# Decay attention and a squared-ReLU FFN: the attention in plain float32 on quarters of the array, one chunk per stretch

## The chip, the cores and the metric

The kernel runs on one core of a Trainium2 chip. The metric is the device time of one execution in microseconds; lower is better. The kernel before was timed three times: 644.21, 644.75 and 645.5 us, median 644.75 us. The profile that is read below comes from an execution of its own.

## The reference

Two operations follow each other. The first is a causal attention with a decay per head, in blocks of 64 positions, for 4 batches, 8 heads, 768 positions and 64 features per head. Its result is the input of a feed-forward network over 3072 tokens.

```python
intra = np.einsum('bhic,bhjc->bhij', qb, kb) * Dmask[None]      # Dmask: lam ** (i - j) for i >= j, else 0
intra = np.einsum('bhij,bhjd->bhid', intra, vb)
inter = np.einsum('bhid,bhde->bhie', qb * lam_pow[None], kv_state)
out[:, :, sl] = intra + inter
kv_state = lam_block[None, :, None, None] * kv_state + np.einsum('bhsd,bhse->bhde', kb_dec, vb)
...
h = np.maximum(x @ w_in, 0.0)        # x: 3072 x 512, w_in: 512 x 2048
return (h * h @ w_out).astype(np.float32)      # w_out: 2048 x 512
```

All inputs and outputs are float32. The FFN's weights arrive as 64-bit words and are turned into float32 on the chip.

## The kernel before

**Tiling.** The kernel works in chunks of 128 positions (`C`), six per batch, 24 in all. `CHUNKS` lists first the four chunks with number 0, one of each batch, and then the rest batch by batch. Three chunks make a token tile of 384 tokens, and there are eight tiles (`TILES`). For each tile the attention of its three chunks writes `x` as a high part `xh` and a low part `xl` in the type float32r, and the FFN then runs 16 steps (`ffn`, one per 128 hidden features).

**The FFN.** One step is twelve matmuls of 384 columns into a PSUM bank `h` (L509: `xh` by `wih`, `xl` by `wih`, `xh` by `wil`), a ReLU and a square on ACT and DVE with a split into `gh` and `gl` (L523 to L530), and nine matmuls of 512 columns that accumulate into three banks `os_`, one per chunk (L515, L516, L518). In the first two tiles the weights of each step are also unpacked and split, on ACT and DVE (`weights`, L265 to L290); from the third tile on they lie ready.

**The attention.** Every chunk is worked in two units of four heads (index `q`). The first nine chunks (`PLAIN`) use float32 matmuls: `unit_plain`, with scores on halves of the array's rows (L319, 64x128 of it), the state's update on halves of its columns (L342), and the result from the state on the whole array (L368) and from the scores on halves of its columns (L371). A float32 matmul shows as two MATMUL records, called passes here. The other 15 chunks (`SPLIT`) use `unit_split`: queries, keys, values, scores and state are each split into a high and a low part in float32r by copies on ACT and subtractions on DVE (L408 to L425, L443, L444); the scores (L432) and the result (L474, L475) are float32r matmuls on the whole array, and the parts of the result are added again on ACT and DVE (L439, L440, L481 to L488). The state's update (L452) is a float32 matmul there, too.

**What sets the order.** `Plan.order` runs once at build time. It takes each operation with an engine, an estimated duration, a key (when it is due) and its buffers, and it hands out buffers and writes one fixed order per engine. Where the estimates leave PE idle in the first 45 us, it puts in filler matmuls on zeros (L241). Buffers for the first phase (`EARLY`) and for the split attention (`LATE`) share the same memory. Two PSUM banks are kept for `h`, and six are shared by the attention and the FFN's accumulators. All loads and stores are issued from SP's queue.

Of the kernel before, what the change touches and what calls it, by code (L numbers as in the profile page):

```python
# [19 lines left out]
P = 128  # L20
# [7 lines left out]
PK = 1536  # L28
# [5 lines left out]

# [6 lines left out]
N_PLAIN = 9  # L41
PLAIN, SPLIT = CHUNKS[:N_PLAIN], CHUNKS[N_PLAIN:]

# [9 lines left out]
class Op:  # L53
    def __init__(self, eng, dur, key, fn, deps, bufs, after, lat, early):
        self.eng, self.dur, self.key, self.fn, self.deps, self.bufs, self.after, self.lat, self.early = (
            eng, dur, key, fn, deps, bufs, after, lat, early)
        self.start = self.end = None


class Plan:  # L60
    LAT = {"PE": 0.25, "ACT": 0.15, "DVE": 0.12, "POOL": 0.12, "SP": 2.0}
    PORT = ("DVE", "POOL")
# [7 lines left out]
    def op(self, eng, dur, key, fn, deps=(), bufs=(), after=(), lat=None, early=None):  # L70
        o = Op(eng, dur, key, fn, [d for d in deps if d is not None], list(bufs), [d for d in after if d is not None], lat or self.LAT[eng], early)
        for b in o.bufs:
            b.left += 1
        self.ops.append(o)
        return o

    def order(self, pe_slow, fill, begin):

# [9 lines left out]
        done, filled, early = [], 0, sum(o.early is True for o in self.ops)  # L88
        while any(ready.values()):
            best = None  # L90
            for e, ops in ready.items():
                can = []
                for o in ops:
                    t = max([free[e]] + [d.end + d.lat for d in o.deps])
                    want = {}
                    for b in o.bufs:
                        if b.slot is None:
                            want[b.kind] = want.get(b.kind, 0) + 1
                    ok = o.early is not False or not early
# [16 lines left out]

# [8 lines left out]
            dur = o.dur * (2.0 if o.eng == "PE" and t < pe_slow else 1.0)  # L125
            o.start, o.end = t, t + dur
# [11 lines left out]
            early -= o.early is True  # L138
# [7 lines left out]


SLOTS = {
# [4 lines left out]
EARLY = ("pnt", "diag0", "diag1", "st", "m")  # L153
LATE = ("pkt", "ab", "ka", "vv", "pp", "z", "zl", "ss0", "ss1")

FIRST, SLOW_STEP, LAG, BEGIN2, SECOND, STEP, PE_SLOW, FILL_END, FILL = 18.0, 6.5, 16, 9.0, 1.5, 4.8, 4.9, 45.0, 0.215

BEHIND = 12  # L160

SPARE = 0.8
# [3 lines left out]
def kernel(ctx: ExitStack, tc: tile.TileContext, pn, pk, lamx, w, out):  # L166
# [3 lines left out]
    phase = ExitStack()  # L170
    plan = Plan()
    for k, n in SLOTS.items():
        plan.kind(k, n)


    shapes = {
        "bank": ([P, 512], F32), "h": ([P, 512], F32),
        "gh": ([P, N], F32R), "gl": ([P, N], F32R), "g": ([P, N], F32), "ob": ([P, DM], F32),
        "s1": ([P, 4, C], F32), "vd": ([P, 4, D], F32), "us": ([P, 2, D], F32), "xr": ([P, 2, C], F32),
        "st": ([P, DM], U64), "m": ([P, DM], F32), "pnt": ([P, 4, 2, P], F32), "diag0": ([P, 2, P], F32), "diag1": ([P, 2, P], F32),  # L180
        "pkt": ([P, PK], F32), "ab": ([P, 4, 2, C], F32R), "ka": ([P, 4, C], F32R), "vv": ([P, 4, 2, D], F32R),
        "pp": ([P, 4, 2, C], F32R), "z": ([P, 2, 2, C], F32), "zl": ([D, 2, 2, C], F32),
        "ss0": ([P, 2, 2, 2, D], F32R), "ss1": ([P, 2, 2, 2, D], F32R), "hold": ([P, 2, D], F32)}
# [6 lines left out]
    make(ps, ("bank", "h"))  # L190
    make(const, [k for k in SLOTS if k not in EARLY + LATE + ("bank", "h", "x")])
    tiles["x"] = [[const.tile([P, NCC, N], F32R, name=f"{n}{i}") for n in ("xh", "xl")] for i in range(SLOTS["x"])]
    rdec = const.tile([P, NP, C], F32, name="rdec")

    flip, zero = tiles["g"][-1][:, 0:P], tiles["ob"][-1]
    lam, ej, ec = (tiles["g"][-1][:, P + 16 * i:P + 16 * i + n] for i, n in enumerate((H + NP, H, NP)))
    mask = const.tile([P, P], F32, name="mask")
# [3 lines left out]
    wol = [const.tile([P, DM], F32R, name=f"wol{f}") for f in range(NF)]  # L201

    wdec = const.tile([P, H], F32, name="wdec")
    lc = const.tile([P, NP], F32, name="lc")
    make(phase.enter_context(tc.tile_pool(name="early", bufs=1)), EARLY)

    def late():
        phase.close()
        pool = ctx.enter_context(tc.tile_pool(name="late", bufs=1, reuse_waits="tile"))
        pool.tile([P, 112], F32, name="space")  # L210
        make(pool, LATE)

        for k in ("ss0", "ss1"):
            for s in tiles[k]:
                nc.gpsimd.memset(s.bitcast(F32), 0.0)
# [4 lines left out]

    def start_tables():
        nc.scalar.dma_start(out=lam, in_=lamx)
        nc.vector.memset(zero, 0.0)
        nc.gpsimd.iota(ej, pattern=[[0, H]], base=MID, channel_multiplier=-1, allow_small_or_imprecise_dtypes=True)
        nc.vector.memset(ec, float(C))

# [4 lines left out]

        for d in tiles["diag0"] + tiles["diag1"]:
            nc.vector.memset(d, 0.0)

        nc.scalar.mul(tiles["g"][-1][:, P + 48:P + 52], zero[:, 0:4], 1.0)

        nc.gpsimd.tensor_tensor(out=wdec, in0=lam[:, 0:H], in1=ej, op=ALU.pow)
        nc.gpsimd.tensor_tensor(out=lc, in0=lam[:, H:H + NP], in1=ec, op=ALU.pow)

    def filler(i):  # L240
        nc.tensor.matmul(tiles["bank"][i][:, 0:P], zero[:, 0:P], zero[:, P:2 * P], start=True, stop=True)  # L241
# [3 lines left out]
    o_start = plan.op("POOL", 1.2, -99, start_tables, early=True)  # L245


    o_pow = plan.op("POOL", 3.0, -98, lambda: None, [o_start], early=True)
    wb, rps = Buf("m"), Buf("bank")

    def turned():
        for n in range(NP):
            nc.tensor.matmul(
                at(rps)[:, n * C:n * C + C], at(wb)[:, n * P:n * P + P], flip, start=True, stop=True)

    o = plan.op("DVE", 0.4, -5, lambda: nc.vector.tensor_copy(
        at(wb).rearrange("p (n h d) -> p n h d", n=NP, h=2), wdec.rearrange("p (n h) -> p n h", h=2).unsqueeze(3).broadcast_to([P, NP, 2, D])),
        [o_pow], [wb], early=True)
    o_turned = o = plan.op("PE", 0.9, 3, turned, [o], [wb, rps], early=True)
    o_rdec = plan.op("DVE", 0.6, 3, lambda: nc.vector.tensor_tensor(  # L260
        out=rdec, in0=at(rps).rearrange("p (n i) -> p n i", n=NP), in1=lam[:, H:H + NP].unsqueeze(2).broadcast_to([P, NP, C]), op=ALU.mult),
        [o], [rps], early=True)


    def weights(f, i, key):  # L265
# [9 lines left out]
        def add(eng, dur, fn, deps, bufs, lat=None):  # L275
            return plan.op(eng, dur, key, fn, deps, bufs, lat=lat, early=True)

        o = plan.op("SP", 1.95, key - 6, lambda: nc.sync.dma_start(out=at(st), in_=w[f, i]), [o_start], [st], early=True)
        o = add("ACT", 0.55, lambda: nc.scalar.activation(at(m), words(1).bitcast(F32), AF.Abs), [o], [st, m])  # L279
        o = add("DVE", 0.35, lambda: nc.vector.tensor_scalar(  # L280
            out=at(m), in0=at(m), scalar1=W_MIN, scalar2=W_MAX, op0=ALU.max, op1=ALU.min), [o], [m])
        o = add("DVE", 0.35, lambda: nc.vector.tensor_scalar(
            out=bits(), in0=bits(), scalar1=3, scalar2=0x3FFFFFF8, op0=ALU.logical_shift_left, op1=ALU.bitwise_and), [o], [m])
        o = add("DVE", 0.6, lambda: nc.vector.scalar_tensor_tensor(
            out=bits(), in0=words(1), scalar=0xC0000000, in1=bits(), op0=ALU.bitwise_and, op1=ALU.bitwise_or), [o], [st, m])
        o = add("DVE", 0.6, lambda: nc.vector.scalar_tensor_tensor(
            out=bits(), in0=words(0), scalar=29, in1=bits(), op0=ALU.logical_shift_right, op1=ALU.bitwise_or), [o], [st, m])
        oh = add("ACT", 0.55, lambda: nc.scalar.copy(hi, at(m)), [o], [m])  # L288
        ol = add("DVE", 0.6, lambda: nc.vector.tensor_tensor(out=lo, in0=at(m), in1=hi, op=ALU.subtract), [oh], [m])
        return oh, ol  # L290


    state, turn = {}, {}

    def in_turn(name, o):

# [5 lines left out]
    half = lambda h: slice(h * 64, h * 64 + 64)  # L302

    def unit_plain(b, c, q, x, col, key, behind=None):

        prs = slice(2 * q, 2 * q + 2)
        t, s1, vd, xr = Buf("pnt"), Buf("s1"), Buf("vd"), Buf("xr")

        def add(eng, dur, dk, fn, deps, bufs, name=None):
            o = plan.op(eng, dur, key + dk, fn, deps, bufs, early=True)  # L310
            return in_turn(name, o) if name else o

        load = add("SP", 1.7, -8, lambda: nc.sync.dma_start(out=at(t), in_=pn[PLAIN.index((b, c)), q]), [behind], [t], "load")
        sc = [Buf("bank"), Buf("bank")]

        def scores():
            for n in range(2):
                for h in range(2):
                    nc.tensor.matmul(at(sc[h])[:, n * C:n * C + C], at(t)[half(h), 0, n], at(t)[half(h), 1, n], start=True, stop=True)  # L319

# [319 lines left out]
```

## Time and profile before

| | |
|---|---|
| median of three runs | 644.75 us (644.21 to 645.5) |
| the profiled execution, span from its first to its last instruction | 643.3 us |
| PE (TensorE) busy | 98% of the span |
| DVE (VectorE) busy | 73% |
| ACT (ScalarE) busy | 58% |
| POOL (GpSimd) busy | 1% |
| DMA | 56.71 MB moved, 88 GB/s in the mean |

The profiled execution's own span is 1.45 us below the median of the timed runs. How to read its views: times are in microseconds from the start of the span, L509 is line 509 of the kernel, and `bank<-gh,woh` means that the instruction writes the tile `bank` and reads `gh` and `woh`. A row of the timeline gives the start, the time until the end of the last instruction of the row, and a count (x8 is eight instructions). Matmuls overlap their neighbours, so the time that a run of them takes on PE is read from its start to the start of the next row; the duration in a row is longer. PEld is the load of a matmul's fixed operand. A number in brackets is idle time before the row, with what ended it.

### The profile page before, as it was taken

To read this page: it belongs to the slowest core of one execution; us is meant where nothing else is said; L and a number is where in the kernel's file an instruction comes from. 1 tells how busy PE (TensorE), PEld (TensorE's weight loads), DVE (VectorE), ACT (ScalarE), POOL (GpSimd) and SP (SyncE) were. 2 spreads that over 40 slices of the span, in tenths; PEclk is the share of its full clock that TensorE was granted. 3 is DMA by queue.
4 is the path that set the end of the run, shared out by engine and by line. 5 is a ranking of instruction groups with operands and counts; after the bars stand their busy time and mean duration, and the time that the engine had idled before them with its cause. 6 is when DMAs were issued, how large, how long until landed. Compare 5 with 4: busy or idle time off the path is not lost.

```text
span 643.3 us, 9671 instructions
## 1 busy us (share of the span) xinstructions
PE 633.4 (98%) x3652; PEld 572.6 (89%) x3652; DVE 470.1 (73%) x1050; ACT 372.5 (58%) x864; POOL 4.7 (1%) x11
## 2 busy tenths in 40 slices
PE   8999999999999999999999999999999999999997
PEld 6788989988899999999999999999899999999996
DVE  4999999844527999579985899759995789742222
ACT  5987777746535666357663666546674566532222
POOL 2000000000000000000000000000000000000000
PEclk9999999999999999999999999999999999999999
DMA  6935555520212121231202122121120121010001
GB/s 238 316 103 170 185 170 204 188 83 34 99 50 98 50 99 49 90 109 49 75 25 98 50 99 99 49 100 48 51 99 34 65 99 50 1 50 1 0 1 49
DMA packets 15165, 56.71 MB, mean 88 GB/s; under 512 B 1808, under 2 KB 1808, under 8 KB 15120
## 3 DMA queue, kind: packets, MB, share of 16 engines
q1 hardware_dynamic: 14976, 56.11, 25.0%
q8 instruction: 28, 0.46, 0.3%
q14 instruction: 17, 0.14, 0.1%
q10 hardware_dynamic: 144, 0.01, 0.0%
HBM read 49.81 MB, written 6.29 MB: 87 GB/s over the span
## 4 chain that ended last, share of the span: by engine, by line
PE 89%; DMA 4%; ACT 3%; DVE 2%; issue 0%; POOL 0%; SPq 0%; ACTq 0%; DVEq 0%; POOLq 0%
PE h L509 38%; PE bank L518 13%; PE bank L515 13%; PE bank L516 13%; PE bank L475 2%; PE bank L474 2%; PE bank L432 2%; DMA pkt<-pk 2%; PE bank L452 2%; PE bank L319 1%; PE bank L371 1%; DMA pnt<-pn 1%; DMA st<-w 1%; DMA g<-lamx 1%; ACT m L279 1%; ACT vd L330 0%
## 5 line engine op out<-in xcount | busy, mean ns | idle before, releaser
L515 PE MATMUL bank<-woh,gh 128*128 128x512 f32 x384 | 151.2, 394 | 1.8 <-ACT gh L526 1.8
L516 PE MATMUL bank<-wol,gh 128*128 128x512 f32 x384 | 150.7, 392 | 0.0
L523 ACT ACTIVATE g<-h 128x384 f32<-128x384 f32 x128 | 62.9, 491 | 131.7 <-PE h L509 131.1
L529 DVE TENSOR_TENSOR g<-g 128x384 f32<-128x384 f32 x96 | 53.4, 556 | 78.9 <-ACT gh L528 78.4
L509 PE MATMUL h<-xh,wih 128*128 128x384 f32 x512 | 110.6, 337 | 0.3 <-ACT wih L288 0.3
L518 PE MATMUL bank<-woh,gl 128*128 128x512 f32 x384 | 110.6, 396 | 0.1
L509 PE MATMUL h<-xl,wih 128*128 128x384 f32 x512 | 109.8, 335 | 0.0
L509 PE MATMUL h<-xh,wil 128*128 128x384 f32 x512 | 109.4, 334 | 0.0
L509 PEld LDWEIGHTS h<-xh,wih 128*128 128x128 f32 x512 | 89.8, 188 | 4.7 <-ACT wih L288 0.6
L509 PEld LDWEIGHTS h<-xl,wih 128*128 128x128 f32 x512 | 91.5, 188 | 0.0
L509 PEld LDWEIGHTS h<-xh,wil 128*128 128x128 f32 x512 | 90.6, 188 | 0.0
L515 PEld LDWEIGHTS bank<-woh,gh 128*128 128x128 f32 x384 | 72.1, 188 | 15.6 <-ACT gh L526 2.7
L518 PEld LDWEIGHTS bank<-woh,gl 128*128 128x128 f32 x384 | 70.1, 188 | 16.9 <-DVE gl L530 2.9
L516 PEld LDWEIGHTS bank<-wol,gh 128*128 128x128 f32 x384 | 72.2, 188 | 12.5
L530 DVE TENSOR_TENSOR gl<-g,gh 128x384 fp32r<-128x384 f32 x128 | 71.0, 555 | 13.1 <-ACT gh L526 9.8
L528 ACT ACTIVATE gh<-g 128x384 fp32r<-128x384 f32 x96 | 50.5, 526 | 2.5
L481 ACT COPY z<-bank 128x256 f32<-128x256 f32 x60 | 22.3, 372 | 36.9 <-PE bank L475 34.3
L482 DVE TENSOR_TENSOR z<-bank,z 128x256 f32<-128x256 f32 x60 | 24.8, 422 | 12.8 <-ACT z L481 11.7
L475 PE MATMUL bank<-pp,vv 128*128 128x256 f32 x120 | 29.8, 281 | 0.0
L474 PE MATMUL bank<-ab,ss 128*128 128x256 f32 x120 | 29.7, 281 | 0.0
L439 ACT COPY s<-bank 128x256 f32<-128x256 f32 x60 | 19.6, 374 | 13.4 <-PE bank L432 13.2
L487 DVE TENSOR_TENSOR xr<-z,zl 64x256 f32<-64x256 f32 x60 | 25.1, 418 | 2.0 <-ACT zl L483 1.0
(79 smaller groups left out, 779.1 us busy)
## 6 DMA issues: line engine op xcount, KB each, us to landing
pkt<-pk SPq DMA_DIRECT2D x30, 768.0 KB, 4.4
st<-w SPq DMA_DIRECT2D x32, 512.0 KB, 3.3
pnt<-pn SPq DMA_DIRECT2D x18, 512.0 KB, 4.9
out<-ob SPq DMA_DIRECT2D x23, 256.0 KB, 2.1
out<-z SPq DMA_DIRECT2D x1, 256.0 KB, 2.0
g<-lamx ACTq DMA_DIRECT2D x1, 6.0 KB, 3.8
```

What stands on the lines that cost most here:

```text
L474: nc.tensor.matmul(y4[:, n], at(ss)[:, n, h].rearrange("p t d -> p (t d)"), at(ab)[:, i], start=n == 0, stop=False, skip_group_check=True)
L475: nc.tensor.matmul(y4[:, n], at(vv)[:, i].rearrange("p t d -> p (t d)"), at(pp)[:, i], start=False, stop=True, skip_group_check=True)
L482: zo.append(add("DVE", 0.36, 2, lambda h=h, part=part: nc.vector.tensor_tensor(out=at(z)[:, h], in0=part(0), in1=at(z)[:, h], op=ALU.add), ...
L487: nc.vector.tensor_tensor(out=at(xr)[half(h)], in0=at(z)[0:64, h], in1=at(zl)[:, h], op=ALU.add)
L509: nc.tensor.matmul(at(h)[:, 0:N], wt[:, cc, :], xt[:, cc, :], start=k == 0, stop=k == 3 * NCC - 1)
L515: nc.tensor.matmul(at(os_[j]), at(gh)[:, sl], woh[f], start=f == 0, stop=False)
L516: nc.tensor.matmul(at(os_[j]), at(gh)[:, sl], wol[f], start=False, stop=False)
L518: nc.tensor.matmul(at(os_[j]), at(gl)[:, sl], woh[f], start=False, stop=f == NF - 1)
L523: orr = plan.op("ACT", 0.45, key, lambda: nc.scalar.activation(at(g), at(h)[:, 0:N], AF.Relu), [o1], [h, g])
L528: ogh = plan.op("ACT", 0.47, key, lambda: nc.scalar.activation(at(gh), at(g), AF.Square), [orr], [g, gh])
L529: og = plan.op("DVE", 0.48, key, lambda: nc.vector.tensor_tensor(out=at(g), in0=at(g), in1=at(g), op=ALU.mult), [orr, ogh], [g])
L530: ogl = plan.op("DVE", 0.48, key, lambda: nc.vector.tensor_tensor(out=at(gl), in0=at(g), in1=at(gh), op=ALU.subtract), [og, ogh], [g, gh, gl])
```

## The change

The split attention goes away: all 24 chunks use float32 matmuls, and every one of them has 64 rows and 64 columns of the array (`half` for rows and for columns). Four matmuls that stand next to each other in the program name the four quarters. A chunk is no longer two units but one. From the seventh chunk on, one `visit` puts the result of the chunk before and the scores and the state's update of the next chunk into one stretch on PE. A stretch has three parts: a first group, the scores between, and a last group. The first and the last group write the same two banks with the rows' halves exchanged, so between them ACT copies one column of the bank to a tile `dot`, and the last group waits for that copy.

The values are scaled in place in the loaded tile (`weighted`), the state is kept without the `diag` layout, and a chunk's masked scores, gate, high part and low part are handled by one or two instructions each on tiles of 512 columns. The first six chunks (`N_ALONE`) are worked alone at the start, by `front` and `back`. The eight PSUM banks are one pool now, `run` keeps the FFN at two banks for its hidden features, and `g` has two buffers instead of three. The planner's estimates are new, and it adds `SWITCH` where PE goes from FFN to attention or back. The FFN computes as before, step for step; its rows of `w_in` and the columns of `x` are permuted alike. A filler is now two float32 matmuls on two quarters.

```diff
-N_PLAIN = 9
-PLAIN, SPLIT = CHUNKS[:N_PLAIN], CHUNKS[N_PLAIN:]
+N_ALONE = 6
...
-    "bank": 6, "h": 2, "x": 2, "gh": 3, "gl": 3, "g": 3, "ob": 2, "hold": 8,
+    "bank": 8, "run": 2, "x": 2, "gh": 3, "gl": 3, "g": 2, "ob": 2,
+    "ka": 2, "qv": 3, "s1": 3, "xr": 1, "hold": 6, "st": 3, "m": 3}
...
     def filler(i):
-        nc.tensor.matmul(tiles["bank"][i][:, 0:P], zero[:, 0:P], zero[:, P:2 * P], start=True, stop=True)
+        for h in range(2):
+            nc.tensor.matmul(tiles["bank"][i][half(h), 0:P], zero[half(0), 0:HC], zero[half(0), P:2 * P], start=True, stop=True)
...
+    def stretch(key, first, between, last, bank, col, deps, bufs):
+        o = plan.op("PE", first[0], key, first[1], deps, bufs, mode="A")
+        dots = plan.op("ACT", 0.2, -50, lambda: nc.scalar.copy(dot, at(bank)[:, col:col + 1]), [o], [bank])
+        if between:
+            o = plan.op("PE", between[0], -50, between[1], [], [], [o], mode="A")
+        return plan.op("PE", last[0], -50, last[1], [dots], bufs, [o], mode="A")
...
+        def update(self, g, u, col, fresh):
+            for q in range(NQ):
+                for r in range(2):
+                    n, bank = 2 * q + (r ^ g), r ^ g
+                    for h in range(2):
+                        mm(
+                            at(u[bank])[half(h), col + q * D:col + q * D + D], at(self.ka)[half(r), 1, n, half(h)], self.vals()[half(r), n, h],
...
+        def scores(self):
+            for n in range(NP):
+                for h in range(2):
+                    for j in range(2):
+                        mm(
+                            at(self.sc[h])[half(j), n * C:n * C + C], at(self.ka)[half(h), 0, n, half(j)], at(self.qv)[half(h), 0, n],
...
+        def result(self, g, y):
+            for q in (range(NQ), reversed(range(NQ)))[g]:
+                for r in range(2):
+                    h = r ^ g
+                    bank, col = y(q, h)
+                    for n in (2 * q, 2 * q + 1):
+                        mm(
+                            at(bank)[half(h ^ (n & 1)), col:col + C], self.vals()[half(r), n, h], at(self.s1[h])[half(r), n],
...
+            for q in range(NQ):
+                for h in range(2):
+                    bank, col = y(q, h)
+                    for n in (2 * q, 2 * q + 1):
+                        mm(
+                            at(bank)[half(h ^ (n & 1)), col:col + C], at(self.old[0])[half(h), n], at(self.qv)[half(h), 0, n],
...
+        def first():
+            prev.result(0, y)
+            if this.more:
+                this.update(0, ys, NQ * C, False)
+        def last():
+            prev.result(1, y)
+            if this.more:
+                this.update(1, ys, NQ * C, False)
```

The order of PE's instructions moves everywhere; two places are shown, as the built programs have them. The first place is one attention block between FFN steps. In the program before, the state's update (`vd`, `pkt`) and the scores (`ab`, `ka`) of one unit stand behind an FFN step, and the results (`ss`, `vv`) come later:

```order
L518 MATMUL bank_65<-woh_136,gl_74 128x512
L452 MATMUL bank_66<-vd_91,pkt_1661 128x128 [waits DMAHW7_49]
L452 MATMUL bank_66<-vd_91,pkt_1661 128x128
L432 MATMUL bank_62<-ab_1663,ka_1664 128x256 x2
L432 MATMUL bank_61<-ab_1663,ka_1664 128x256 [waits Activation_49]
L432 MATMUL bank_61<-ab_1663,ka_1664 128x256
L509 MATMUL h_67<-xh_95,wih_105 128x384 x4
```

In the changed program a whole visit stands there. The rows below are its end: the scores of the next chunk (`qv`, `ka`, 16 matmuls), then the last group of the results (`s`, `qv`), and the FFN's accumulation after it:

```order
L273 MATMUL bank_66<-qv_147,ka_143 64x128 x2
L273 MATMUL bank_67<-qv_147,ka_143 64x128 x2
L273 MATMUL bank_66<-qv_147,ka_143 64x128 x2
L273 MATMUL bank_67<-qv_147,ka_143 64x128 x2
L273 MATMUL bank_61<-s_0_148,qv_146 64x128 [waits Activation_49]
L273 MATMUL bank_61<-s_0_148,qv_146 64x128
L273 MATMUL bank_62<-s_2_150,qv_146 64x128 x2
L273 MATMUL bank_61<-s_0_148,qv_146 64x128 x2
L273 MATMUL bank_62<-s_2_150,qv_146 64x128 x2
L458 MATMUL bank_64<-woh_113,gh_133 128x512
```

What moved: two blocks per chunk and per pair of heads have become one block per chunk, and inside it one group waits for ACT. The second place is the start, at the first FFN step. Before, the step stands between results of the sixth chunk, with one run of fillers (`bank<-ob`) behind it:

```order
L371 MATMUL bank_63<-s_0_88,vd_90 64x128 x4
L509 MATMUL h_67<-xh_95,wih_101 128x384 x4
L509 MATMUL h_67<-xl_96,wih_101 128x384 x4
L509 MATMUL h_67<-xh_95,wil_117 128x384 x4
L368 MATMUL bank_61<-pnt_173,diag_1_177 128x128 x2
L371 MATMUL bank_61<-s_1_89,vd_91 64x128 x4
L342 MATMUL bank_66<-vd_91,pnt_173 64x64 x4
L241 MATMUL bank_64<-ob_79 128x128 x8
```

In the changed program the step stands behind the fourth chunk's scores and a run of fillers (`bank<-ob`, two matmuls per filler), and the rest of the fourth chunk follows it:

```order
L273 MATMUL bank_64<-qv_145,ka_144 64x64 x2
L219 MATMUL bank_66<-ob_142 64x128 x26
L452 MATMUL bank_66<-xs,wih_69 128x384 x8
L452 MATMUL bank_66<-xs,wil_85 128x384 x4
L273 MATMUL bank_67<-s_2_150,qv_145 64x128 x2
L273 MATMUL bank_68<-s_0_148,qv_145 64x128 x2
```

What moved: six chunks stood before the first FFN step but for their last results, now four do, and the fillers grew. In PE's whole order the fillers before number 22 matmuls, those of the changed program 160, of which the first 40 stand ahead of the first chunk and all but 24 ahead of the first FFN step.

More of the change, by code (lines that the diff above doesn't have):

```diff
@@ L27 @@
 NQ = NP // 2
-PK = 1536
+HC = C // 2
 W_MIN = struct.unpack("<f", struct.pack("<I", 897 << 20))[0]
@@ L188, in make @@
             tiles[k] = [pool.tile(*shapes[k], name=f"{k}{'_' if k[-1].isdigit() else ''}{i}") for i in range(SLOTS[k])]
[L190 to L197, printed above, removed]
+    make(ps, ("bank",))
     wih = [const.tile([P, NCC, P], F32R, name=f"wih{f}") for f in range(NF)]
@@ L201 @@
     wol = [const.tile([P, DM], F32R, name=f"wol{f}") for f in range(NF)]
-    wdec = const.tile([P, H], F32, name="wdec")
-    lc = const.tile([P, NP], F32, name="lc")
[L205 to L215, printed above, removed]
+    make(const, [k for k in SLOTS if k not in ("bank", "x", "run")])
+    rdec = const.tile([P, NCC, C], F32, name="rdec")
+    mask = const.tile([P, P], F32, name="mask")
+    xs = const.tile([P, XOFF + 2 * SLOTS["x"] * NCC * N], F32R, name="xs")
+    tiles["x"] = [[xs[:, XOFF + (2 * i + t) * NCC * N:XOFF + (2 * i + t + 1) * NCC * N].rearrange("p (c i) -> p c i", c=NCC) for t in range(2)] for i in range(SLOTS["x"])]
+    dot = const.tile([P, 1], F32, name="dot")
+    wdec = const.tile([P, 2 * H], F32, name="wdec")
+    lc = const.tile([P, NP], F32, name="lc")
+    flip, zero = tiles["g"][-1][:, 0:P], tiles["ob"][-1]
+    lam, ej, ec = (tiles["g"][-1][:, P + a:P + a + n] for a, n in ((0, 2 * H + 2 * NP), (32, 2 * H), (48, NP)))
     def at(b):
@@ new lines, with visit @@
+    state = {}
+    def visit(prev, this, x, col, key, per):
+        ys = [Buf("bank"), Buf("bank")]
+        old = prev.old
+        y = lambda q, h: (ys[h], q * C)
+        this.old = state.get(this.b)
+        def first():
[6 more added lines that the diff above has]
+                this.update(1, ys, NQ * C, False)
+        part = 0.25 * this.more
+        o = stretch(key, ((0.9 if old else 0.46) + part, first), (0.9, this.scores), (0.46 + part, last), ys[1], NQ * C + D if this.more else C,
+                    [this.o_ka, this.o_qv] + this.o_vd + prev.o_vd + prev.o_s1 + ([old[1]] if old else []),
+                    [this.ka, this.qv, prev.qv, x] + prev.s1 + this.sc + ys + ([old[0]] if old else []))
+        if this.more:
+            this.passed_on(o, ys, NQ * C, key)
+        this.masked(o, key)
+        return prev.gated(o, ys, key, key + per, x, col, this.o_u if this.more else ())
@@ new lines @@
+    chunks = []
+    for i in range(len(CHUNKS)):
+        ti, j = i // NT, i % NT
+        if i < N_ALONE:
+            key = i * CHUNK if ti == 0 else BEGIN2 + (i - NT) * CHUNK
+        else:
+            k = ti - 1 if j else max(ti - 2, 1)
+            key = begin[k] + per[k] * ((0.5, 4.5, 8.5) if k == 1 and ti == 2 else (12.5, 3.5, 8.0))[j]
+        ch = Chunk(i, key)
+        ch.load(key - (8 if i < N_ALONE else 14))
+        ch.weighted(key - (1 if i < N_ALONE else 6))
+        chunks.append(ch)
@@ L581 @@
+    for i, ch in enumerate(chunks):
+        ti, j = divmod(i - 1, NT)
+        if i <= N_ALONE:
+            ch.front(ch.key)
+            if i < N_ALONE:
+                ready[i // NT] += ch.back(ch.key + 0.2, xs_[i // NT], (i % NT) * C)
+        else:
+            ready[ti] += visit(chunks[i - 1], ch, xs_[ti], j * C, ch.key, STEP)
+    ti, j = len(TILES) - 1, NT - 1
+    ready[ti] += chunks[-1].back(begin[ti - 1] + 12.5 * per[ti - 1], xs_[ti], j * C)
+    for ti, cs in enumerate(TILES):
         os_ = [Buf("bank") for _ in cs]
```

399 lines of the change are left out of this document (150 added, 249 removed), and 3 rows, old and new, of the table SLOTS.

## The prediction

> **What bounds the kernel now.** I read the page's busy times first, then the busy times by stage, then the chain that ended last, then PE's timeline in the stages that the change touches. The first row below is the page's, the others are stages (length; then busy time of PE, PEld, DVE and ACT with instruction counts; the fourth last number is POOL's, then the granted clock, DMA share, GB/s).
>
> ```profile
> PE 633.4 (98%) x3652; PEld 572.6 (89%) x3652; DVE 470.1 (73%) x1050; ACT 372.5 (58%) x864; POOL 4.7 (1%) x11
> 16.00:33.40 17.40, 16.07 (x212) 13.11 (x210) 16.44 (x44) 16.79 (x60) 0.00 (x0) 1.00 0.86 297
> 42.00:120.00 78.00, 77.73 (x397) 70.88 (x396) 74.52 (x146) 56.94 (x114) 0.00 (x0) 1.00 0.55 190
> 180.00:530.00 350.00, 350.00 (x1935) 321.17 (x1935) 281.35 (x643) 207.01 (x470) 0.00 (x0) 1.00 0.21 73
> ```
>
> From 42 us on PE has no gaps worth the name, so every microsecond taken off PE's row comes off the time, as long as the other engines keep up. DVE is close behind while weights are unpacked (74.52 of 78 us) and at 80% later. Before 33 us everything is busy at once.
>
> How long is the FFN alone? The chain's end, where no attention is left, has two steps between neighbouring rows of this kind:
>
> ```profile
> 597.92 4.18 PE h L509 x24
> 622.84 4.18 PE h L509 x24
> ```
>
> Six steps take 24.92 us, 4.153 each, and 128 steps take 531.6 us. The rest is the start, the attention and the end:
>
> ```profile
> 1.52 2.93 PE L241 MATMUL bank<-ob 128*128 128x128 f32 x12 [1.52 <-DVE ob L223]
> 10.13 1.17 PE L253 MATMUL bank<-g,m 128*128 128x128 f32 x8
> 11.24 0.66 PE L371 MATMUL bank<-s,vd 128*64 128x128 f32 x8
> 42.30 0.87 PE L509 MATMUL h<-xh,wih 128*128 128x384 f32 x4
> 639.22 0.40 PE L518 MATMUL bank<-woh,gl 128*128 128x512 f32 x1
> ```
>
> At 42.30 the second FFN step begins, so the start costs 42.30 - 4.15 = 38.15 us beside FFN work. The last matmul starts at 639.22 and takes 0.23 us; from there the last copy and store take 643.3 - 639.45 = 3.85 us. Between lie 643.3 - 38.15 - 531.6 - 3.85 = 69.7 us of attention and waits. The change acts on these and on the start.
>
> **What the removed attention costs.** A split unit in the steady stage:
>
> ```profile
> 288.68 0.28 PE L474 MATMUL bank<-ab,ss 128*128 128x256 f32 x1
> 289.61 0.86 PE L518 MATMUL bank<-woh,gl 128*128 128x512 f32 x3
> 292.36 0.64 PE L432 MATMUL bank<-ab,ka 128*128 128x256 f32 x4
> 292.83 0.86 PE L509 MATMUL h<-xh,wih 128*128 128x384 f32 x4
> 311.92 0.60 PE L452 MATMUL bank<-vd,pkt 128*128 128x128 f32 x4
> 312.83 0.86 PE L509 MATMUL h<-xh,wih 128*128 128x384 f32 x4
> ```
>
> Eight result matmuls take 0.93 us, four score matmuls 0.47, and update and scores together 0.91, so the update is 0.44. Thirty units, 24 of them with an update, make 30 x 1.40 + 24 x 0.44 = 52.6 us. The six plain units of the third tile run between FFN steps, too:
>
> ```profile
> 133.70 0.39 PE L516 MATMUL bank<-wol,gh 128*128 128x512 f32 x1
> 134.02 0.72 PE L319 MATMUL bank<-pnt 64*128 64x128 f32 x8
> 134.66 0.97 PE L518 MATMUL bank<-woh,gl 128*128 128x512 f32 x3
> 135.47 0.86 PE L509 MATMUL h<-xh,wih 128*128 128x384 f32 x4
> 137.56 0.60 PE L368 MATMUL bank<-pnt,diag 128*128 128x128 f32 x4
> 138.09 0.66 PE L371 MATMUL bank<-s,vd 128*64 128x128 f32 x8
> 139.40 0.50 PE L515 MATMUL bank<-woh,gh 128*128 128x512 f32 x1 [0.18 <-ACT gh L526]
> 173.33 0.50 PE L515 MATMUL bank<-woh,gh 128*128 128x512 f32 x1 [0.49 <-ACT gh L526]
> ```
>
> The scores lengthen 133.70 to 135.47 (1.77 us) by 1.77 - 0.23 - 0.69 = 0.85 us; the rest of a unit takes 1.2 to 1.4, so six units cost about 13. That leaves 69.7 - 52.6 - 13 = 4.1 us, waits like the two in brackets (0.18, 0.49) and late starts.
>
> **What the new attention costs.** No row shows quarters. These narrow windows show two halves of the columns, first for 128 moving columns and then for 64 (with the whole run of 16), and the loads' row last:
>
> ```profile
> 138.09 0.33 PE L371 MATMUL bank<-s,vd 128*64 128x128 f32 x2
> 138.47 0.28 PE L371 MATMUL bank<-s,vd 128*64 128x128 f32 x2
> 138.58 0.64 PE L342 MATMUL bank<-vd,pnt 128*64 128x64 f32 x16
> 138.58 0.23 PE L342 MATMUL bank<-vd,pnt 128*64 128x64 f32 x2
> 138.99 0.23 PE L342 MATMUL bank<-vd,pnt 128*64 128x64 f32 x2
> 138.09 0.20 PEld L371 LDWEIGHTS bank<-s,vd 128*64 128x64 f32 x4
> ```
>
> Two passes always start together, and four loads are done in 0.20 us. Four pairs of 128 columns start from 138.09 to 138.47, so a round takes 0.109 us once 0.05 us for the first load is taken off; eight pairs of 64 columns start from 138.58 to 138.99, 0.058 us each. A product on the whole array (the two of L368, 137.56 to 138.09, less 0.10 of draining) takes 0.215, two passes of 0.109. So a half runs at full speed beside the other half. Halves of the rows do so too: eight passes of L319 between 134.02 and 134.66 leave 0.44 us for four rounds once 0.2 are taken for the first load and the draining. Rows and columns each split without a price, and I expect both together to do so: rounds of four passes at 0.109 and 0.058 us. The other end of the range is that no more than two passes run at once.
>
> Per chunk, then: scores are 16 products, 32 passes, 8 rounds, 0.87 us; results from the scores the same, 0.87; results from the state 8 products, 0.44; the update 16 products of 64 columns, 8 rounds of 0.058, 0.46. Changing the array's layout costs about 0.15 on the way in (draining, first load) and 0.21 on the way back, by the rows from 133.70 to 138.09, so 0.36 us per stretch.
> - 13 visits with an update: 2.64 + 0.36 = 3.00, together 39.0.
> - 4 visits without: 2.18 + 0.36 = 2.54, together 10.2.
> - the seventh chunk's front: 0.87 + 0.46 + 0.36 = 1.7; the last chunk's back: 1.31 + 0.36, and 0.45 for its wait for the `dot` copy, which nothing covers: 2.1.
>
> That is 53.0 us in place of 52.6 + 13 = 65.6. The copy to `dot` is short by the nearest row, a copy of four columns:
>
> ```profile
> L235 ACT ACTIVATE g<-ob 128x4 f32<-128x4 f32 x1 | 0.2, 208 | 0.0
> ```
>
> In a visit the scores (0.87 us) stand over the way from PE to ACT and back. That way needs 0.2 us of copy and some 0.2 of hand-over, so it is hidden; if ACT is inside a ReLU or square, it is late by up to 0.5 us, and then the last group and all FFN matmuls queued behind it wait. Of the 4.1 us of waits I keep 1.5, since they were ends of ACT and DVE work and both engines get less: per chunk the masks, state, gate, low part and scaling are nine DVE instructions,
>
> ```profile
> L441 DVE TENSOR_TENSOR s<-s,mask 128x512 f32<-128x512 f32 x30 | 20.7, 689 | 0.5
> L488 DVE TENSOR_TENSOR xr<-xr,rdec 128x256 f32<-128x256 f32 x30 | 12.7, 425 | 1.0
> ```
>
> four of the first size, three of the second and two short ones, 4.6 us, where a split chunk has eight of the first size alone (L418, L420, L441 and L444 in two units). The bounds for these waits are 0 and 18 stretches x 0.5 = 9 us.
>
> **The start.** Both kernels load 1 MB per chunk here, so DMA asks the same (297 GB/s in the row from 16 us on). But PE runs its order, and that holds 80 fillers of two matmuls now, against 22. At the clock of the first microseconds a pass takes 0.24 us (12 in 2.9); from 11.24 on it takes 0.109. Twenty fillers at 0.48 and 60 at 0.22 are 22.8 us. Six chunks are 4 x 2.2 + 2 x 2.64 = 14.1; the transposes of the decay table (L253) 0.9; five changes of layout 1.8; 1.5 before the first; 1 us of waits that no filler covers. Sum 42.1 us, against 38.15 now. If the clock rises earlier it is 39, if ACT and DVE (94 to 96% busy in this stage before) are late it is 46.
>
> **The sum.** 42.1 + 531.6 + 53.0 + 1.5 + 3.85 = 632.05 us for a span of 643.3. The profiled span lies 1.45 us below the median of the runs; with that the time is 633.5, and I say 633 us against 644.75.
>
> **Rivals.**
> - *Passes are issued too slowly for four quarters.* PE starts a pass at best every 0.029 us in the rows (two per 0.058). A round of four short passes would then take 0.116: 8 rounds x 0.058 = 0.46 us more for each of 20 chunks with an update, 9 us, and with 0.007 more on each long round (20 rounds, 24 chunks) another 3: 646. Against it: the passes of a pair start within 0.01 us. [...] Chance 0.10.
> - *The new wait decides.* ACT reaches `dot` late, or a stretch that holds four of eight banks (three more are the FFN's accumulators) keeps the next hidden bank back. At 0.3 us in each of 18 stretches the time is 638, at 0.5 it is 642. For it: one hidden bank is left during a visit. Against it: ACT has lost the split's copies, and its next ReLU can run while the visit does. Chance 0.13.
> - *Only two quarters run at once.* Then every round counts twice: 45.7 us of passes between FFN steps and 14.1 at the start come on top, 633 + 60 = 693 us, slower. It decides from the point where rounds are 20% longer (12 of 60 us), at 0.130 us instead of 0.109. For it: nothing in this trace runs more than two. Against it: each half took nothing from the other, in loads and in passes. Chance 0.12.
>
> **How the numbers follow.** The forecast as summed has 0.65; with the bounds of the start (39 to 46) and of small waits it lies between 627 and 640. The issue rival reaches 646 and the wait rival 642. The range 626 to 646 leaves out the third rival and tails, under 2 in 10. About 0.2% is what a measurement of this kernel can tell from no change. Faster: 0.65 + 0.12 of the wait rival + 0.07 of the issue rival = 0.84; the same 0.03; slower 0.13.
>
> **What would show it.** Right: in a visit, four MATMUL records start within some 0.03 us, and rounds follow at 0.109 and 0.058; a visit takes 2.6 to 2.7 us from its first matmul to its last; PE has no gap after the start; FFN steps between visits take 4.15 us. The start is right if the second FFN step's work begins some 4 us later than before. Wrong: rounds of 0.13 or more, PE idle in front of the last group with ACT's `dot` as the releaser, or a start beyond 46 us.

## The result, and the profile after

The changed kernel takes 634.07 us (median of 4 runs, 633.6 to 636.91), the kernel before 644.48 in the same comparison: a ratio of 0.984, 95% interval 0.9814 to 0.9866, so about 10 us faster. The profiled execution took 633.6 us and has a span of 631.85.

The page's row of busy times:

```profile
PE 624.1 (99%) x5512; PEld 566.8 (90%) x5512; DVE 304.5 (48%) x606; ACT 210.6 (33%) x441; POOL 4.7 (1%) x9
```

The same three stages as before (length; busy time of PE, PEld, DVE, ACT with counts; then POOL, granted clock, DMA share, GB/s):

```profile
16.00:33.40 17.40, 16.81 (x463) 16.28 (x456) 13.48 (x32) 8.08 (x25) 0.00 (x0) 1.00 0.75 277
42.00:120.00 78.00, 76.28 (x486) 68.76 (x487) 68.97 (x138) 49.66 (x98) 0.00 (x0) 1.00 0.48 162
180.00:530.00 350.00, 350.00 (x3050) 318.40 (x3049) 141.77 (x279) 90.10 (x186) 0.00 (x0) 1.00 0.14 51
```

PE is full again; DVE's busy time has halved in the steady stage (281 to 142 us of 350), ACT more than halved. PE's row went down by 9.3 us, the span by 11.5. One visit, on the timeline (start, length, instructions; `s,qv` and `qv,hold` are results, `qv,ka` updates and scores):

```profile
163.11 0.67 PE L273 MATMUL bank<-s,qv 64*64 64x128 f32 x16
163.60 0.62 PE L273 MATMUL bank<-qv,hold 64*64 64x128 f32 x16
164.03 1.29 PE L273 MATMUL bank<-qv,ka 64*64 64x64 f32 x48
164.56 0.16 ACT L279 COPY dot<-bank 128x1 f32<-128x1 f32 x1 [5.21 <-PE bank L273]
165.14 0.62 PE L273 MATMUL bank<-s,qv 64*64 64x128 f32 x16
165.58 0.41 PE L273 MATMUL bank<-qv,ka 64*64 64x64 f32 x16
165.92 0.44 PE L452 MATMUL bank<-xs,wih 128*128 128x384 f32 x1
```

From 163.60 to 164.03 lie 16 passes of 128 columns, four rounds: 0.108 us each. From 164.03 to 165.14 lie four short rounds and eight long ones: 4 x 0.058 + 8 x 0.109 = 1.10. The four passes of a round start 0.007 us apart in the single records. The visit takes 2.81 us from its first pass to the FFN's next matmul, and no PE row has a wait in brackets. The start, for comparison:

```profile
8.59 1.49 PE L219 MATMUL bank<-ob 64*64 64x128 f32 x12
9.67 0.48 PE L273 MATMUL bank<-qv,ka 64*64 64x64 f32 x4
10.09 2.77 PE L273 MATMUL bank<-qv,ka 64*64 64x64 f32 x60
12.79 2.08 PE L229 MATMUL bank<-g,m 128*128 128x128 f32 x8
14.80 1.20 PE L219 MATMUL bank<-ob 64*64 64x128 f32 x18
18.15 3.33 PE L219 MATMUL bank<-ob 64*64 64x128 f32 x58
51.69 0.50 PE L458 MATMUL bank<-woh,gh 128*128 128x512 f32 x1 [1.51 <-ACT gh L469]
```

The first chunk's front lasts 3.1 us (9.67 to 12.79), where the seventh chunk's, of the same 64 passes, takes 1.5, and the decay table's eight transposes take 2.0 us. Fillers run for 3 us in one piece. Of the first 60 us, 45.6 have gone to other things than FFN matmuls (these counted at 0.1733 and 0.2267 us), against 38.3 in the kernel before. And the FFN alone, two pairs of steps:

```profile
586.50 1.55 PE L452 MATMUL bank<-xs,wih 128*128 128x384 f32 x8
594.75 1.55 PE L452 MATMUL bank<-xs,wih 128*128 128x384 f32 x8
```

Two steps take 8.25 us, 4.126 each, where they took 8.31 before. With the terms of the prediction the 11.5 us of the span come apart like this: the attention between FFN steps gives 12.6 (53.0 for 65.6), the FFN's steps 3.4, the waits 2.8 (1.3 left of 4.1), and the start takes back 7.3 (45.6 for 38.3).

### The profile page after: what moved, and what is told of

It reads as the page before. It is cut to its first block, busy times and chain, and to the rows that moved or that the text cites. A ratio compares the mean times of both kernels' runs of the same rounds, so it can differ in the third digit from the quotient of the medians.

```text
span 631.8 us, 12563 instructions
## 1 busy us (share of the span) xinstructions
PE 624.1 (99%) x5512; PEld 566.8 (90%) x5512; DVE 304.5 (48%) x606; ACT 210.6 (33%) x441; POOL 4.7 (1%) x9
## 4 chain that ended last, share of the span: by engine, by line
PE 97%; DVE 1%; DMA 1%; ACT 0%; issue 0%; DVEq 0%; ACTq 0%
PE bank L452 42%; PE bank L461 14%; PE bank L458 14%; PE bank L459 14%; PE bank L273 10%; PE bank L219 3%; DMA out<-ob 1%; PE bank L229 0%; DVE ob L491 0%; DVE s L353 0%; DVE gl L473 0%; DVE hold L369 0%; DVE xr L401 0%; DVE xr L491 0%; DVE hold L375 0%
## 5 line engine op out<-in xcount | busy, mean ns | idle before, releaser
L452 PE MATMUL bank<-xs,wih 128*128 128x384 f32 x1024 | 199.8, 337 | 0.0
L452 PEld LDWEIGHTS bank<-xs,wih 128*128 128x128 f32 x1024 | 179.6, 188 | 6.8 <-issue 0.5
L466 ACT ACTIVATE g<-bank 128x384 f32<-128x384 f32 x128 | 63.0, 493 | 285.5 <-PE bank L452 285.1
L452 PE MATMUL bank<-xs,wil 128*128 128x384 f32 x512 | 109.6, 336 | 0.0
L452 PEld LDWEIGHTS bank<-xs,wil 128*128 128x128 f32 x512 | 90.6, 188 | 0.0
L273 PE MATMUL bank<-qv,ka 64*64 64x128 f32 (+1 forms) x1408 | 40.2, 252 | 0.0
L273 PEld LDWEIGHTS bank<-qv,ka 64*64 64x64 f32 x1408 | 36.3, 137 | 0.4 <-DVE ob L491 0.4
L353 DVE TENSOR_TENSOR s<-bank,mask 128x512 f32<-128x512 f32 x48 | 32.4, 681 | 3.7 <-PE bank L273 3.7
L273 PE MATMUL bank<-s,qv 64*64 64x128 f32 x768 | 31.9, 276 | 0.2 <-ACT dot L279 0.2
L219 PE MATMUL bank<-ob 64*64 64x128 f32 x320 | 24.3, 308 | 2.1 <-DVE ob L206 1.5
```

Source lines behind the costliest of these rows:

```text
L219: nc.tensor.matmul(tiles["bank"][i][half(h), 0:P], zero[half(0), 0:HC], zero[half(0), P:2 * P], start=True, stop=True)
L273: nc.tensor.matmul(*args, **kw, skip_group_check=True)
L353: self.o_s1 = [in_turn("mask", plan.op("DVE", tt(512), key, lambda h=h: nc.vector.tensor_tensor(out=at(self.s1[h]), in0=at(self.sc[h]).rea ...
L452: nc.tensor.matmul(at(h)[:, 0:N], wt[:, cc, :], xt[:, cc, :], start=k == 0, stop=k == 3 * NCC - 1)
L466: orr = plan.op("ACT", 0.49, key, lambda: nc.scalar.activation(at(g), at(h)[:, 0:N], AF.Relu), [o1], [h, g, run])
```

## The experiments

Each is an edit of the changed kernel; its times are compared with 634.07 through the kernel before, which ran beside it each time (644.2 to 645.4).

**Do four quarters need neighbouring products on four quarters?** The first two runs change only the order of a chunk's 16 score products.

```
-for n in range(NP):
-    for h in range(2):
-        for j in range(2):
+for h in range(2):           # pairs
+    for n in range(NP):
+        for j in range(2):
```

> The score products of a chunk are put in another order (rows' half outermost, then heads, then the columns' half), so that only two neighbouring products lie on different quarters; same products, same results. Theory (four quarters run at once because PE starts passes in order and finds four neighbouring products on four idle quarters): a chunk's scores take 16 rounds of two passes instead of 8 of four, 1.74 us for 0.87, 24 x 0.87 = +21 us over the changed kernel's 634, so 655, and a visit is 3.87 us long. Rival (each quarter has a queue of its own that is filled far ahead): no change, 634. Second rival (the four-at-once speed never came from the quarters but from products being small): no change either.

Measured: 646.78 us, ratio 1.0026 (1.0005 to 1.0047). A visit:

```profile
166.05 0.67 PE L273 MATMUL bank<-s,qv 64*64 64x128 f32 x16
166.98 1.45 PE L273 MATMUL bank<-qv,ka 64*64 64x64 f32 x42
168.16 0.33 PE L273 MATMUL bank<-s,qv 64*64 64x128 f32 x2
169.35 1.66 PE L452 MATMUL bank<-xs,wih 128*128 128x384 f32 x8
```

The visit lasts 3.30 us (166.05 to 169.35) instead of 2.81: +0.49, not +0.87. The single records show why. Two quarters start a pass each at 167.209, .321, .430, .539 and .648, and the other two begin at 167.661, when the first two still have three passes each to start. So two quarters work alone for 0.45 us, where the theory has 0.87 and the rivals 0. The theory was half right, and both rivals fell. Over 24 stretches with scores 0.49 us make 12 of the 12.7 us that the run takes more than the changed kernel. The second run puts four products in a row on one quarter:

```
+for h in range(2):           # one quarter at a time
+    for j in range(2):
+        for n in range(NP):
```

> The score products with the heads innermost: four products in a row lie on the same quarter, then four on the next. Same products and results. The run with two quarters in turn showed that the other two quarters began when the first two had three passes each left to start. Theory (PE hands products out in order, and a quarter holds about three passes that have not started): the second quarter begins 0.45 us after the first, the third at 0.9, the fourth at 1.35, its eight passes end at 2.2; the last group follows into the idle quarters early, so a visit costs 1.1 to 1.4 us more, 24 chunks 26 to 34 us, 660 to 668. Rival A (no such store at all, products strictly one after the other where the quarter repeats): scores 3.5 us instead of 0.87, +63, about 697. Rival B (stores deep enough for a whole chunk): no change, 634.

Measured: 672.41 and 684.62 us, two runs and so no interval. The profile is of the longer one, where passes took the long time of the start until 52 us; this visit lies far behind that:

```profile
233.34 0.67 PE L273 MATMUL bank<-s,qv 64*64 64x128 f32 x16
234.26 2.42 PE L273 MATMUL bank<-qv,ka 64*64 64x64 f32 x45
236.42 0.33 PE L273 MATMUL bank<-s,qv 64*64 64x128 f32 x3
237.60 0.50 PE L458 MATMUL bank<-woh,gh 128*128 128x512 f32 x1
```

It takes 4.27 us, +1.46. In the single records the second, third and fourth quarter begin their scores 0.44, 0.93 and 1.42 us after the first, near the 0.45, 0.9 and 1.35 that were expected. The visit is a little longer than the 1.1 to 1.4 us more that were expected, and far from +2.6. The shorter run is 38 us over the changed kernel, just beyond the 660 to 668 expected; 24 x 1.46 = 35 of them are this.

**What is a stretch worth, and what hides the dot copy?** Three runs. In the first the scores go ahead of a stretch's first group:

```
-o = plan.op("PE", first[0], key, first[1], ...)
+o = plan.op("PE", first[0] + (between[0] if between else 0), key,
+            lambda: [f[1]() for f in (between, first) if f], ...)
...
-if between:
-    o = plan.op("PE", between[0], -50, between[1], [], [], [o], mode="A")
```

> The scores of a stretch go ahead of its first group instead of between the first and the last, so nothing stands over the way from PE to ACT's dot copy and back; the same products. Theory (the copy of 0.16 us and the hand-overs are hidden by the 0.87 us of scores, with some 0.35 us to spare): each of 17 visits and of the 7 fronts pays 0.3 to 0.4 us of PE idle in front of its last group, +5 to +8 us, so 639 to 642, and rows with dot as the releaser appear in every visit. Rival (PE finds the copy done anyway, since the group before drains long enough): within 1 us of the changed kernel.

Measured: 640.71 us, ratio 0.9942 (0.9918 to 0.9966): the time came as expected, the mechanism did not.

```profile
167.40 0.62 PE L273 MATMUL bank<-s,qv 64*64 64x128 f32 x16
167.83 0.62 PE L273 MATMUL bank<-qv,hold 64*64 64x128 f32 x16
168.38 1.67 PE L450 MATMUL bank<-xs,wih 128*128 128x384 f32 x8
169.88 0.86 PE L450 MATMUL bank<-xs,wil 128*128 128x384 f32 x4
170.67 0.67 PE L273 MATMUL bank<-s,qv 64*64 64x128 f32 x16
```

The planner saw the wait and put an FFN group into it, so no visit waits for dot; it pays two more changes of layout instead. After 62 us there are 36 stretches where there were 20, and from 100 us to the end it takes 4.2 us longer: 0.26 us for each of 16. So this run prices a stretch, not the copy. The next splits all chunks in two:

```
-ready[ti] += visit(chunks[i - 1], ch, xs_[ti], j * C, ch.key, STEP)
+ready[ti] += chunks[i - 1].back(ch.key, xs_[ti], j * C)
+ch.front(ch.key + 0.2)
```

> All chunks' fronts (scores and update) and backs (results) are stretches of their own, as those of the first six are; same products. Theory (what a stretch costs is the change of layout, 0.36 us, and the wait for dot where no scores cover it): 17 visits become two stretches each, 17 x 0.36 = +6 us, and 17 uncovered waits of 0.35, or another FFN group in the wait with two more changes of 0.36, 6 to 12 us: 646 to 652 in all, about what the kernel before takes. Rival (changes of layout are free, since loads of the next weights run beside): within 1 us of 634.

Measured: 648.68 us, ratio 1.005 (1.003 to 1.0071), slower than the kernel before. The time is inside what was expected. There are 54 stretches after 62 us, 34 more, and 14.5 us more from 100 us on: 0.43 each. The two runs lie on both sides of the 0.36 that the prediction took. The third makes the copy longer:

```
-lambda: nc.scalar.copy(dot, at(bank)[:, col:col + 1])
+lambda: [nc.scalar.copy(dot, at(bank)[:, col:col + 1]) for _ in range(8)]
```

> The copy to dot is made eight times in a row instead of once, and the planner still counts it as 0.2 us; everything else is as in the changed kernel. Theory (the way from PE to ACT and back is hidden by the 0.87 us of scores with 0.35 us to spare): if eight copies take 0.8 to 1.3 us, the last group of each stretch with scores waits 0.3 to 0.8 us, 24 x 0.3 to 0.8 = 7 to 19 us, less what the fillers of the start would have taken: 640 to 651, with PE idle in front of the last group and dot as its releaser in every visit. Rival (PE does not wait for the copy, it is released by something else): no change, 634. Second rival (ACT's other work, late by the longer copies, holds up the FFN): idle in front of the second FFN product's rows instead.

Measured: 662.66 us, ratio 1.0272 (1.0235 to 1.0308). A visit, and the copies in it:

```profile
218.44 0.67 PE L273 MATMUL bank<-s,qv 64*64 64x128 f32 x16
219.36 1.29 PE L273 MATMUL bank<-qv,ka 64*64 64x64 f32 x48
219.84 1.50 ACT L279 COPY dot<-bank 128x1 f32<-128x1 f32 x8 [0.25 <-PE bank L273]
221.39 0.67 PE L273 MATMUL bank<-s,qv 64*64 64x128 f32 x16 [0.74 <-ACT dot L279]
222.22 0.50 PE L458 MATMUL bank<-woh,gh 128*128 128x512 f32 x1
```

The copies end at 221.34 and the last group starts at 221.39, so this is the wait that the group obeys. They are 1.34 us longer than one copy; the visit is 0.97 longer (3.78). The scores therefore hid one copy with 0.37 us to spare, as expected. The total was mis-set. Eight copies take 1.50 us and not 0.8 to 1.3, so each stretch with scores pays 0.97 and not 0.3 to 0.8: from 100 us on 17.7 us for 18 of them. The other 11.5 us of the profiled run lie before 100 us, where backs wait for the copies, too, and where the granted clock fell to 0.66 from 20 to 30 us; what each of these took is not shown.

**Why is an FFN step 0.027 us shorter?** The change also puts the FFN's inputs into one tile, 16 words (64 bytes) off its beginning:

```
-XOFF = 16
+XOFF = 0
```

> Only the place of the FFN's input tiles in SBUF moves, by 64 bytes (the offset of 16 words is taken away). Theory (an FFN step takes 4.126 us after the change and 4.153 before because of where tiles lie in SBUF): the step goes back towards 4.15, +2 to +4 us, about 637. Rival (the step became shorter for another reason, such as which instructions ACT and DVE run beside it): within 0.5 us, step still 4.126.

Measured: 638.39 us, ratio 0.9899 (0.9862 to 0.9937).

```profile
583.71 1.57 PE L452 MATMUL bank<-xs,wih 128*128 128x384 f32 x8
592.02 1.57 PE L452 MATMUL bank<-xs,wih 128*128 128x384 f32 x8
```

Two steps take 8.31 us again, exactly the kernel before's. In the single records the same matmuls are slower in both (the third and fourth of a pair of steps with 177 and 185 ns, with the offset 173 and 169; five accumulations of 228 to 236, with it 227). So 128 x 0.027 = 3.4 us of the change's gain hang on these 64 bytes. Why is not shown: the five accumulations, which do not read these inputs, change as well, and the small tiles that the kernel makes behind the inputs may move with them. The profiled run is 5.8 us longer than the changed kernel's; the other 2.4 lie in its start (the row of 51.69 stands at 54.23), where the granted clock was 0.83 from 30 to 40 us.

**What sets the start?** Three runs: no fillers, fillers on the whole array, and a planner that knows when loads land.

```
-PE_SLOW, FILL_END, FILL, SWITCH = 4.9, 45.0, 0.215, 0.18
+PE_SLOW, FILL_END, FILL, SWITCH = 4.9, 0.0, 0.215, 0.18
```

> The planner puts in no fillers at all. Theory (fillers in PE's fixed order stand in front of chunks 2 to 5, whose loads had landed about 2 us before PE got to them): the first FFN step starts 3 to 6 us earlier, 628 to 631. Rival A (the clock needs the fillers: without them the first chunks run at the slow clock, and every pass there takes twice as long): the six chunks cost up to 14 us more, but partly while PE would have waited for loads, 634 to 642. Rival B (loads and their buffers set the pace of the six chunks, the fillers only fill): no change, within 1 us.

Measured: 629.58 us, ratio 0.976 (0.9726 to 0.9794), 5 us faster without a single filler:

```profile
18.13 0.44 PE L273 MATMUL bank<-s,qv 64*64 64x128 f32 x4 [1.69 <-DVE s L353]
19.21 2.32 PE L273 MATMUL bank<-qv,ka 64*64 64x64 f32 x42
48.31 0.50 PE L458 MATMUL bank<-woh,gh 128*128 128x512 f32 x1 [1.52 <-ACT gh L469]
```

```profile
20.00:30.00 10.00, 7.12 (x161) 0.71 0.71 257
```

PE waits 4 us for masks in all, and the clock does fall: it is granted at 0.71 from 20 to 30 us (the number behind PE's count in the window's row), and 42 passes take 2.32 us, where 42 such passes at 14.41 us, with the clock granted at 1.00, take 1.25. Still the FFN's row comes at 48.31 instead of 51.69. The fillers on quarters stood in the chunks' way by more than the clock is worth. Next:

```
-for h in range(2):
-    nc.tensor.matmul(tiles["bank"][i][half(h), 0:P], zero[half(0), 0:HC], zero[half(0), P:2 * P], start=True, stop=True)
+nc.tensor.matmul(tiles["bank"][i][:, 0:P], zero[:, 0:P], zero[:, P:2 * P], start=True, stop=True)
```

> A filler is one product on the whole array (128 rows and columns) instead of two on two of its four quarters; their number and places stay. Theory (half an array of work lets the clock rise later: the chunks' passes became short at 14.6 us with the quarter fillers and at 10.7 in the kernel before with whole ones): the first chunk's front and the transposes of the decay table run at the short times, 2 to 3 us earlier, but the next chunk waits for its loads, so of this 0 to 2 us are left: 632 to 634. Rival (the clock needs a time, not a load): no pass gets shorter, 634; and fillers that change the array's layout before every chunk cost 12 x 0.3 = 3.6 us more: 637.

Measured: 630.12 us, ratio 0.9762 (0.9748 to 0.9777). Filler passes per window (PE, then PEld), first of this kernel, then of the changed one, where two passes run beside each other:

```profile
2.00:4.00 2.00, 2.00 (x11) 2.00 (x10) 1.00 0.78 284
5.00:7.00 2.00, 2.00 (x20) 2.00 (x19) 1.00 1.03 422
```

```profile
2.00:4.00 2.00, 2.00 (x22) 2.00 (x21) 1.00 0.79 294
7.00:9.00 2.00, 2.00 (x22) 2.00 (x20) 1.00 0.94 385
```

On the whole array a pass goes from 0.214 to 0.112 us at 4.4 us, three microseconds after the first. In the changed kernel the passes on two quarters still take 0.214 us when the front begins at 9.67, and so do the front's passes at 12 us, though PE never pauses. What follows is early by that much:

```profile
8.13 2.26 PE L272 MATMUL bank<-qv,ka 64*64 64x64 f32 x64 [0.49 <-ACT qv L306]
10.32 1.16 PE L228 MATMUL bank<-g,m 128*128 128x128 f32 x8
48.52 0.50 PE L457 MATMUL bank<-woh,gh 128*128 128x512 f32 x1 [1.52 <-ACT gh L468]
```

The gain of 4 us is twice what I expected, because the next chunk's loads do not set a pace of their own: they wait for the front to release its buffers. Issues of `ka` (SP's queue), the changed kernel first, this one second:

```profile
12.93 0.33 SPq L295 DMA_DIRECT2D ka<-ka  x1
18.39 0.33 SPq L295 DMA_DIRECT2D ka<-ka  x1
```

```profile
10.43 0.33 SPq L294 DMA_DIRECT2D ka<-ka  x1
15.03 0.33 SPq L294 DMA_DIRECT2D ka<-ka  x1
```

They are 2.5 and 3.4 us earlier, so the delay of the first front is handed on to the chunks behind it. Third:

```
-plan.op("SP", 1.75, early, ...), plan.op("SP", 1.95, key - 6, ...)
+plan.op("SP", 1.28, early, ..., lat=2.5), plan.op("SP", 1.28, key - 6, ..., lat=2.5)
```

> The planner is told that loads of 512 KB follow each other at 1.28 us and land 2.5 us later, as the trace shows (landings 1.25 to 1.3 us apart), instead of 1.75 or 1.95 and 2.0; nothing else. Theory (PE's fixed order in the start is laid out for loads that come later than they do, and fills the time with 58 filler products at a stretch): shorter stretches of fillers, first FFN step 2 to 4 us earlier, 630 to 632. Rival (loads are issued no earlier, since their buffers come free only when PE is through with a chunk): within 1 us of 634. Against the theory: the planner may order chunks so that PE waits for masks, +1 to +2.

Measured: 628.99 us, ratio 0.9742 (0.9725 to 0.976). The longest run of fillers behind the first chunk:

```profile
32.52 2.18 PE L220 MATMUL bank<-ob 64*64 64x128 f32 x36
```

The fillers are nearly as many (79 for 80), but in shorter runs (36 passes where 58 stood), and the wait of 1.5 us for `gh` is gone.

**Do they add up?** Both together; then a filler counted as 0.30 us, so that 56 are placed; then the decay's power in two pieces:

```
+FILL = 0.30
...
-nc.gpsimd.tensor_tensor(out=wdec, in0=lam[:, 0:2 * H], in1=ej, op=ALU.pow)
+nc.gpsimd.tensor_tensor(out=wdec, in0=lam[:, 0:H], in1=ej[:, 0:H], op=ALU.pow)
+nc.gpsimd.tensor_tensor(out=wturn, in0=lam[:, H:2 * H], in1=ej[:, H:2 * H], op=ALU.pow)
```

> Both changes of the start together: the planner's loads at 1.28 us with 2.5 us to land, and fillers on the whole array. Theory (two separate causes: passes at the long time until the clock rises, and an order laid out for late loads): alone they gave 630 and 629 where the changed kernel takes 634; they overlap where both shorten the same stretch, so 626 to 629. Rival (both work on one and the same wait, the loads' buffers): 629, as with the planner's numbers alone.

> As the run with the planner's loads and whole-array fillers, and the planner counts a filler as 0.30 us instead of 0.215 (56 fillers instead of 79), so that a stretch of fillers ends some 30% ahead of the work that it waits for. Theory (each filler that PE still has to run when the chunk's data is there delays it): up to 1 us less than with all fillers, 625 to 628. Rival A (all gaps are now covered by loads or masks, not by fillers): no change. Rival B (gaps between fillers let the clock fall as without fillers): +1 to +3.

> As the run with 56 whole-array fillers and the planner's loads, and GpSimd raises the decay table in two pieces: the 8 columns that weight the values first, the 8 for the transposed table after them (one instruction of 16 columns took 2.90 us; 8 columns took 1.64 us in the kernel before). Theory (the first chunk's weighting on ACT, and with it PE's first pass, the release of the first buffer and every later load, waits for this power: ACT sat until 7.97 us, PE for 1.76 us): the first front 1.2 us earlier and the start shorter by 0.7 to 1.2 us, 627.2 to 627.7. Rival (the masks, the unpacking of weights or the stores of the chunks set the pace further on): under 0.3 us, 628.4.

Measured: 629.43 us, ratio 0.9761 (0.9742 to 0.9779); 628.41, 0.9751 (0.9728 to 0.9775); 629.40, 0.9767 (0.9747 to 0.9788). They do not add up: each of the six versions of the start, 628.4 to 630.1, beats the changed kernel by 4 to 6 us and the one before by some 15, and the intervals do not tell them apart. In the profiled runs the time that is not FFN work, counted to 100 us, still falls (45.8 us changed kernel, 42.6 whole fillers, 42.2 planner, 41.8 both, 40.3 fewer fillers, 39.2 split power), but the last step shows in one run of five only (626.76, the profiled one; the others 629.05 to 629.76). The mean granted clock was 1.000 in that run and 0.994 to 0.997 in the other four. With 56 fillers the clock does fall in places, as its Rival B said: the profile shows 0.90 from 5 to 10 us and 0.88 from 10 to 20. That this is what limits the others fits, but no run separates it.

## Why the prediction was right, and where it was lucky

The time came out at 634.07 for 633, and the terms tell how:

- *Rounds of four at 0.109 and 0.058 us.* Right. The 17 visits are 13 of 2.81 and 4 of 2.34 us; with some 0.09 us before and 0.11 in the first FFN matmul after, 3.00 and 2.54, as summed. The front took 1.70 and the last back 2.03 (in two stretches, with an FFN group in its wait) for 1.7 and 2.1; together 53.0.
- *Waits 1.5 us after the start.* 1.3 are left over. The dot copy costs nothing where scores cover it. The way from PE to ACT and back, put at 0.4 us (half of it the author's estimate of the hand-overs), takes 0.5: of the scores' 0.87 us the eight copies found 0.37 to spare.
- *The start at 42.1.* Wrong by 3.5, inside its bounds of 39 to 46. The step that failed is "from 11.24 on it takes 0.109": that time was the one of the kernel before, whose fillers fill the array. Here the fillers fill half of it, and the front and the transposes still ran at the long pass (+1.6 and +1.1 us), and the 1 us of uncovered waits was 2.3 (1.5 for `gh`, 0.6 among fillers, 0.2 for dot). The time of the fillers themselves, 22.8, came out as 22.5. The run with whole-array fillers removes most of the first part (front 2.2 us, transposes 1.2), the planner's run most of the second.
- *128 steps of 4.153 us.* Too much by 3.4. That it cancels the start's 3.5 is luck. The term was carried over as untouched, but the change moves the FFN's inputs by 64 bytes; the run with the offset at 0 brings the old step back, and took 638.39 us.
- *The tail* was 3.88 for 3.85.

Of the rivals, slow issue fell with the first visit: the short round is 0.058 us, and the four passes of a round start 7 ns apart. "Only two quarters run at once" is false, too, but an order of products can come near it: with the scores in pairs alone it cost 12.7 us, with one quarter at a time 38. The new wait did not decide, with the margin above; eight copies show what it costs when it does.

## What to carry to other kernels

Quarters of the array are worth what their order lets them be: send neighbouring products to different quarters (the scores in pairs took 0.49 us more per visit here, one quarter at a time 1.46), keep them in one stretch (each further stretch took 0.26 to 0.43 us here), and put independent work over any round trip to another engine (0.5 us to ACT and back here). Whether fillers shorten the passes is read from the time per pass: here it was short from 4.4 us on with fillers on the whole array, and still long at 9.67 with fillers on two quarters. A filler also stands in a fixed order: one placed for data that comes earlier than planned is a delay. No fillers at all (629.58 us) and fillers on the whole array (630.12) were equally good here. A term that a change "does not touch" must be checked for addresses, too (64 bytes were 3.4 us here).

## What the runs showed of the hardware

- The time per pass fell at different moments, and what sets the moment is not shown. With fillers on the whole array a pass went from 0.214 to 0.112 us at 4.4 us, 2.9 us after the first. With fillers on two quarters in their place, passes still took 0.214 us at 9.67, 8.2 us after the first, though PE had not paused. In seven profiles with fillers on quarters the passes become short between 12 and 16 us, after the first front has begun to use all four quarters; with eight copies this happens at about 12.3 us, ahead of any whole-array pass. In the kernel before, the fillers on the whole array (1.52 to 4.41 us) take 0.214 us each after the first, the passes on halves behind them, with a pause of 1.17 us, take that long until 9.8 us, and from 10.4 us on a pass takes 0.112. With one quarter at a time, in the longer of the two runs, passes stay long until 52 us, though PE has no pause from 10 to 50. The granted clock's column says 1.00 where it was read (the changed kernel from 5 to 60 us, the mean of the whole run with one quarter at a time); only the time per pass shows it.
- Passes on different quarters can start out of the program's order: in the run with pairs the last group's first pass starts at 168.16 us, the last of the scores ahead of it in the program at 168.48. There the second two quarters begin at 167.661 us, while the first two have three passes each to start; with one quarter at a time the others begin 0.44, 0.93 and 1.42 us after the first.
- 64 bytes in the place of the FFN's input tiles change some float32r matmuls by up to 16 ns (185 to 169) and a step by 0.027 us (4.153 to 4.126).
- GpSimd's power takes 2.90 us for 16 columns (the changed kernel) and 1.64 for 8 (the run with the power in two pieces, and the kernel before).
